# Pooled attention and two MLPs on one core: block 0's queries in 1 KB runs, five plain steps, and a plan with trace durations

## The chip, the cores and the metric

The kernel runs on 1 core of one Trainium2 chip. The metric is the device time of one execution in microseconds (us); three executions were timed, and the median counts. One further execution was profiled.

## The reference, cut to what matters

Attention over keys and values that are averaged in groups of 8, then two MLPs. Everything is float32.

```python
# q, k, v: 8 batches, 8 heads, 576 positions, 64 wide
k_p, v_p = mean of k and v over groups of 8 positions        # 72 pooled positions
attn = softmax(q @ k_p.T / 8);  x = attn @ v_p               # x: 4608 tokens x 512
h = x @ w_in                                                  # 512 -> 2048
g = where(h >= 1, h, where(h <= -1, 0, (h + 1) ** 2 / 4))
y = g @ w_out                                                 # 2048 -> 512
out = (sigmoid(y @ w_gate) * (y @ w_val)) @ w_out2            # 512 -> 1536 -> 512
```

## The kernel before, in words

The 4608 tokens are nine blocks of 512. Blocks 0 to 6 go through the first MLP one after the other, each in 16 steps (one step is 128 columns of `w_in` and the matching 128 rows of `w_out`). Blocks 7 and 8, and then the second MLP for all blocks but the first, are done in pairs with Strassen's seven products (lines 1000 to 1350). Attention for block j+1 and later is woven in between the steps of the blocks before.

**Precision.** Nearly every product is three matmuls (lines 607 to 611): each operand is split into a high part in fp32r and a low part (value minus high), and high times high, high times low and low times high are added in PSUM. The high part is a ScalarE copy, the low part a VectorE subtraction (lines 531 to 545, recorded at L534 and L543). The raw weights come from memory as 64-bit words whose two halves are put together by two ScalarE and four VectorE instructions per weight tile (lines 556 to 600).

**Plain steps.** In block 0, steps below `PLAIN = 12` (line 241) skip the split for the second product: `g` and the `w_out` rows stay float32 and one float32 matmul (line 772; the profile records it as two) takes the place of three. From step 12 on the step splits `w_out` into a `wj` buffer and `g` into two halves, so ScalarE makes two more copies and VectorE two more subtractions per step (lines 746 to 756).

**Block 0's attention** runs per pair of heads p = 0 to 3. `pooled` (line 319) loads keys and values, sums groups of 8 on VectorE or TensorE, turns the keys on TensorE (line 360) and scales them into `kt`. `unit` (line 385) loads the queries of the two heads with two DMAs (line 401) into a tile ordered (token, head, width), so each run that lands is 64 floats, 256 bytes; turns them with four TensorE transposes (line 407); makes scores (line 436), the maximum (line 445), exponentials with their sums (line 448), the division (line 455), turns the weights (line 470), multiplies with the values (line 508) and splits the result into x (lines 515 and 522). Block 0's q tiles of pairs 2 and 3 borrow the two `wj` buffers. All DMAs from SyncE go through one queue (SP), in the order of issue; GpSimd's own go through POOL's.

**Order of the work.** Nothing is written out by hand: every instruction is an `Op` with an engine, an estimated cost, a key (a due time) and its data dependencies, and `Plan.issue` (line 126) walks through a model of the engines, taking at each point the ready operation with the smallest key. An `Op` may have two ways, on ScalarE or VectorE, and the plan takes the one that ends first. The costs and the constants at the head of the file (lines 25 to 56) therefore change only the order of issue on each engine and that choice, not what one instruction does. A DMA ends in the model when its last byte lands (line 195).

**Rows out.** At the end of a first-MLP block the four accumulator banks are copied to two staging tiles (`out_rows`, line 621): the first is the single `st` tile, the second a tile of the `raw` pool (two buffers), which also takes the raw `w_out` rows, the second MLP's weights on their way to memory and the tiles of `prepare1`. From block 4 on, x is loaded from memory (line 706) into the `x` pool of eight tiles, which by then holds those of the two blocks before.

Of the kernel before, what the change touches and what calls it, by code (L numbers as in the profile page):

```python
# [27 lines left out]
RATE0, RAMP = 240e3, 30.0  # L28

START = 30.0  # L30
STEP1 = 6.35
# [16 lines left out]
PREP2 = 0.5  # L48
AHEAD_COPY = 8.0
UNIT0, UNIT_STEP = 14.0, 3.2  # L50
PREP0, PREP_STEP = (30.5, 68.5), 4.5
AHEAD_RELOAD = 30.0
BEHIND_V = 14.96
# [21 lines left out]
class Plan:  # L75
# [50 lines left out]
    def issue(self):  # L126
# [19 lines left out]
        while n:  # L146
# [42 lines left out]
            if o.bytes:  # L189
# [5 lines left out]
                free[eng], o.end = max(t, lanes[-8] + lat), lanes[-1]  # L195
# [12 lines left out]
def pooled_attention_two_mlps(  # L208
# [30 lines left out]
    PE_SUMS = 1  # L239
    DVE_VALUES = (2, 3)  # L240
    PLAIN = 12
# [37 lines left out]
    def fixed(t):  # L279
        return Buf(tile=t)  # L280
# [23 lines left out]

    T0, S1, S2 = START, STEP1, 7.8

    def due1(s):
        return T0 + S1 * s
# [10 lines left out]
    def pooled(b, p, T):  # L319
# [27 lines left out]
        load(k, ks, T - 20)  # L347
# [9 lines left out]
        else:  # L357
            kp = buf_a("kp", 2, [C, 2, D])
            pool_sum(T, ks, kp, b == 0)
            op(PE, 0.06 if b else 0.25, T + 1, lambda: nc.tensor.transpose(  # L360
                out=pt.t[:, 0:C], in_=kp.t.rearrange("c h d -> c (h d)"), identity=ident.t[:C, :C]),
                r=[kp, ident], w=[pt], share=C / P)


        op((ACT, DVE), (0.21, 0.22), T + 2, (
            lambda: nc.scalar.activation(out=kt.t[:, 0:C], in_=pt.t[:, 0:C], func=AF.Copy, scale=att_scale),
            lambda: nc.vector.tensor_scalar(
                out=kt.t[:, 0:C], in0=pt.t[:, 0:C], scalar1=att_scale, scalar2=None, op0=ALU.mult)), r=[pt], w=[kt])
        load(v, vs, T - (10 if b else AHEAD_V))
# [15 lines left out]
    def unit(j, p, T):  # L385
# [10 lines left out]
        if first:  # L396

            qb = buf_a("q", 2, [P, NT4, 2, D]) if p < 2 else Buf(wj_p, "wj", 2, [P, 2, TB])
            qs = Src(qb) if p < 2 else Src(qb, lambda t: t[:, 0].rearrange("p (t h d) -> p t h d", t=NT4, h=2))
            for h in range(2):  # L400
                op(SP, 0.475, T - 20, lambda h=h: nc.sync.dma_start(
                    out=qs()[:, :, h], in_=q[0, h0 + h, 0:TB].rearrange("(s t) d -> s t d", t=NT4)), w=[qb], nbytes=TB * D * 4)
            ptq = bank("acc")

            def transposes():
                for t in range(NT4):
                    nc.tensor.transpose(out=ptq.t[:, P * t:P * t + P],
                                        in_=qs()[:, t].rearrange("s h d -> s (h d)"), identity=ident.t)
            op(PE, 1.05, T, transposes, r=[qb, ident], w=[ptq])
# [3 lines left out]
        else:  # L413
# [8 lines left out]
            for f in range(4):  # L422
                op(SP, 0.475, T - 20, lambda f=f: load_q(f), w=[qs], nbytes=TB * 256, dmas=len(segs))
# [7 lines left out]

        def scores():
            for r0 in range(0, TB, D):
# [5 lines left out]
        op(PE, 1.15 if first else 0.6, T + 3, scores, r=[qT] + [kts[b % 2, p] for _, _, b, _ in segs], w=scs)  # L439
        for h in range(2):  # L440
# [6 lines left out]
            for t in range(NT4):  # L447
                op(ACT, 0.3 if first else 0.52, T + 5, lambda t=t, h=h, view=view, mx=mx: nc.scalar.activation(
                    out=e.t[:, t, h, 0:C], in_=view()[:, t], func=AF.Exp,
                    bias=mx.t[:, t:t + 1], scale=1.0,  # L450
                    accum_out=sums.t[:, t, h:h + 1]), r=[sc, mx], w=[e, sums], after=[zeros])
# [10 lines left out]
        if first:  # L462

            flat = Src(aT, lambda t: t.rearrange("c a h t j -> c (a h t j)"))
            for h in range(2):
# [5 lines left out]
                op(PE, 1.02, T + 9, transposes, r=[e, ident], w=[pt])  # L471
# [39 lines left out]
        op(PE, 1.05 if first else 0.86 + 0.25 * (len(segs) > 1 and j % 2), T + 18 - AHEAD_PX * first, values,  # L511
# [879 lines left out]
```

## Time and profile before

| | us |
|---|---|
| median of the three runs | 1690.37 |
| lowest and highest run | 1690.08, 1693.66 |
| the profiled execution's own time | 1693.15 |
| its span, first to last instruction | 1691.4 |
| TensorE busy in the span | 1667.2 (99%) |
| VectorE busy | 1168.6 (69%) |
| ScalarE busy | 967.8 (57%) |
| GpSimd busy | 238.3 (14%) |
| mean granted TensorE clock (1 is full) | 0.996 |

Busy time is the union of the instructions' recorded spans; instructions on one engine overlap a little, so the distance from start to start is what one costs in a dense stretch. The shares are means over stages with different limits, and the kernel has four: block 0's attention (until about 33 us), block 0's steps (until about 146 us), the other blocks of the first MLP, and the Strassen pairs.

### The profile page before, as it was taken

Reading aid. Unit: us, or ns where it says so; the run is one execution under the profiler, and the core shown is the slowest. Engines: PE = TensorE matmul, PEld = TensorE weight load, DVE = VectorE, ACT = ScalarE, POOL = GpSimd, SP = SyncE. Lnnn points to the kernel's source line nnn. Section 1 sums busy time; section 2 is a strip of 40 time slices with the busy share of each in tenths; the row PEclk is TensorE's granted clock in tenths of the full one; section 3 lists DMA queues with packets and bytes.
Section 4 is the critical chain, followed back from the end, with each engine's and each line's share of the span. In section 5 each row is a group of like instructions: output and inputs, shape, how many; then the busy total and the mean of one; then the engine's idle time right before and its main releaser. Section 6 shows DMA issues by size and latency. Waiting matters only on the chain.

```text
span 1691.4 us, 26119 instructions
## 1 busy us (share of the span) xinstructions
PE 1667.2 (99%) x8484; PEld 1323.8 (78%) x8484; DVE 1168.6 (69%) x2166; ACT 967.8 (57%) x2140; POOL 238.3 (14%) x338
## 2 busy tenths in 40 slices
PE   7999999999999999999999999999999999999998
PEld 5657777777777777788888888878888888888886
DVE  7988767878787878846778856574448445744476
ACT  6767556676676668643466735454435454544344
POOL 1224323333433222100000002100000000000000
PEclk8999999999999999999999999999999999999999
DMA  8889867777877656547887879997889788977774
GB/s 218 246 250 244 203 138 203 230 217 195 233 201 191 175 162 211 175 159 303 326 275 239 292 237 370 360 343 215 234 257 304 211 238 274 280 194 205 206 219 135
DMA packets 308647, 396.07 MB, mean 234 GB/s; under 512 B 133664, under 2 KB 173856, under 8 KB 306976
## 3 DMA queue, kind: packets, MB, share of 16 engines
q1 hardware_dynamic: 270848, 285.97, 57.1%
q0 software_dynamic: 37664, 108.44, 20.6%
q8 instruction: 68, 1.11, 0.3%
q14 instruction: 67, 0.55, 0.1%
HBM read 272.11 MB, written 112.72 MB: 228 GB/s over the span
## 4 chain that ended last, share of the span: by engine, by line
PE 89%; DMA 5%; DVE 3%; SPq 1%; ACT 1%; issue 1%; POOL 0%; DVEq 0%; POOLq 0%; ACTq 0%
PE acc L609 12%; PE h L609 12%; PE acc L611 12%; PE acc L610 12%; PE h L610 11%; PE h L611 11%; PE a L609 5%; PE a L611 5%; PE a L610 5%; PE a L508 2%; DMA kv<-in_k_dram 2%; PE a L436 1%; PE acc L772 1%; DMA raw<-in_moe_w_out_dram 1%; SPq L487 1%
## 5 line engine op out<-in xcount | busy, mean ns | idle before, releaser
L834 DVE TENSOR_TENSOR g<-win,g 128x512 fp32r<-128x512 f32 x168 | 114.8, 689 | 113.1 <-ACT g L833 111.7
L609 PE MATMUL h<-x,win 128*128 128x512 f32 x448 | 183.4, 409 | 2.1 <-DVE t L746 2.1
L611 PE MATMUL h<-x,win 128*128 128x512 f32 x448 | 175.1, 391 | 1.3 <-DVE win L543 1.3
L610 PE MATMUL h<-x,win 128*128 128x512 f32 x448 | 175.3, 391 | 0.4 <-DVE x L522 0.4
L833 ACT CAST g<-win 128x512 fp32r<-128x512 f32 x168 | 104.3, 624 | 111.8 <-PE acc L611 90.5
L609 PE MATMUL acc<-g,wj 128*128 128x512 f32 x400 | 161.3, 403 | 0.0
L610 PE MATMUL acc<-g,wj 128*128 128x512 f32 x400 | 156.5, 391 | 0.0
L611 PE MATMUL acc<-g,wj 128*128 128x512 f32 x400 | 156.2, 391 | 0.0
L609 PE MATMUL acc<-g,wo 128*128 128x512 f32 x360 | 140.1, 389 | 0.7 <-ACT g L833 0.7
L611 PE MATMUL acc<-g,wo 128*128 128x512 f32 x360 | 140.1, 389 | 0.0
L610 PE MATMUL acc<-g,wo 128*128 128x512 f32 x360 | 140.1, 389 | 0.0
L609 PE MATMUL h<-x,ws 128*128 128x512 f32 x336 | 131.3, 391 | 0.4 <-ACT h L1335 0.4
L610 PE MATMUL h<-x,ws 128*128 128x512 f32 x336 | 131.0, 390 | 0.2 <-DVE x L829 0.2
L611 PE MATMUL h<-x,ws 128*128 128x512 f32 x336 | 130.8, 389 | 0.0
L741 ACT ACTIVATE t<-h,half 128x512 f32<-128x512 f32 x112 | 77.2, 689 | 89.0 <-PE h L611 88.0
L609 PEld LDWEIGHTS h<-x,win 128*128 128x128 f32 x448 | 84.1, 188 | 28.4 <-issue 6.0
L611 PEld LDWEIGHTS h<-x,win 128*128 128x128 f32 x448 | 84.1, 188 | 20.7 <-DVE win L543 2.6
L610 PEld LDWEIGHTS h<-x,win 128*128 128x128 f32 x448 | 84.2, 188 | 19.2 <-issue 2.4
L609 PEld LDWEIGHTS acc<-g,wj 128*128 128x128 f32 x400 | 75.1, 188 | 24.3 <-issue 7.4
L611 PEld LDWEIGHTS acc<-g,wj 128*128 128x128 f32 x400 | 75.1, 188 | 16.8 <-DVE wj L543 0.3
L534 ACT CAST wj<-wout_f 128x512 fp32r<-128x512 f32 x100 | 61.8, 620 | 43.4 <-PE acc L611 37.1
L610 PEld LDWEIGHTS acc<-g,wj 128*128 128x128 f32 x400 | 75.1, 188 | 14.6 <-DVE f L590 0.2
(308 smaller groups left out, 4062.0 us busy)
## 6 DMA issues: line engine op xcount, KB each, us to landing
ws<-seven SPq DMA_DIRECT2D x412, 256.0 KB
wo<-seven_o SPq DMA_DIRECT2D x144, 256.0 KB
seven<-f POOLq DMA_DIRECT2D x64, 256.0 KB, 3.8
seven<-wa POOLq DMA_DIRECT2D x8, 1792.0 KB, 7.7
seven_o<-wo POOLq DMA_DIRECT2D x42, 256.0 KB, 5.8
w<-f POOLq DMA_DIRECT2D x36, 256.0 KB, 4.2
wo<-seven SPq DMA_DIRECT2D x36, 256.0 KB
win<-in_moe_w_in_dram SPq DMA_DIRECT2D x16, 512.0 KB
```

The source lines that it names most:

```text
L436: nc.tensor.matmul(out=scs[h].t[r0 % P:r0 % P + D, r0 // P * C:r0 // P * C + C], lhsT=qT.t[D * h:D * h + D, r0:r0 + D], rhs=kts[b % 2, p]. ...
L487: op(SP, 0.65, T + 10, lambda a=a, bl=bl, n=n: nc.sync.dma_start(out=aT.t[32 * bl:32 * bl + n, a].rearrange("c h t j -> c (h t j)"), in_=a ...
L508: nc.tensor.matmul(out=px.t[D * h:D * h + D, lo:hi], lhsT=vps[b % 2, p].t[:, h], rhs=rhs, start=True, stop=True)
L534: ACT: (0.52, lambda: nc.scalar.copy(out=dst.t[:, 0], in_=src())),
L609: nc.tensor.matmul(out=o, lhsT=wh, rhs=xh, start=start, stop=False, skip_group_check=more)
L610: nc.tensor.matmul(out=o, lhsT=wh, rhs=xl, start=False, stop=False, skip_group_check=more)
L611: nc.tensor.matmul(out=o, lhsT=wl, rhs=xh, start=False, stop=stop, skip_group_check=more)
L741: op(ACT, 0.69, Tg, lambda t=t, hps=hps: nc.scalar.activation(out=t.t, in_=hps.t, func=AF.Relu, bias=half.t, scale=0.5), r=[hps, half], w=[t])
L772: nc.tensor.matmul(out=accs[c].t, lhsT=wj.t[:, c * P:(c + 1) * P], rhs=g.t, start=m == 0, stop=m == M1 - 1)
L833: op2(ACT, cost, key, lambda: nc.scalar.copy(out=out_hi(), in_=val()), r=[src, b], w=[b])
L834: op2(DVE, cost, key + 0.5, lambda: nc.vector.tensor_tensor(out=out_lo(), in0=val(), in1=out_hi().bitcast(F32), op=ALU.subtract), r=[src, ...
```

## The change

- Block 0's queries are loaded with one DMA per pair of heads, into a tile ordered (head, token, width), in which the four tokens of a partition are one run of 1 KB. A transpose of 128 columns then holds two tokens of one head, not two heads of one token, so the keys are also put, by two matmuls, into a second set of 72 columns with the heads exchanged, and `first_scores` picks for each head and token parity the half that lies on the same rows. The number of score matmuls (16 per pair), of transposes and of exponentials stays.
- `PLAIN` goes from 12 to 5: steps 5 to 11 of block 0 get the split and three matmuls.
- The rows of blocks 0 to 4 are staged in two tiles of the `x` pool; those of block 5 both in `st`, one after the other. The reload of x for block j waits for the copies of block j-2's rows.
- The plan's costs are set to other values, a DMA ends 0.7 us later in the model, and the constants at the head get new values. Loops that add idle matmuls are there with a count of 0.

```diff
+LATE = 0.7
-RATE0, RAMP = 240e3, 30.0
+RATE0 = 240000.0
+RAMP = 23.86
-START = 30.0
-STEP1 = 6.35
+START = 30.317
+STEP1 = 6.332
...
-                free[eng], o.end = max(t, lanes[-8] + lat), lanes[-1]
+                free[eng], o.end = max(t, lanes[-8] + lat), lanes[-1] + LATE
...
-    PLAIN = 12
+    PLAIN = 5
...
-            kts[i, p] = fixed(ac.tile([P, P], F32, name=f"kt{i}{p}"))
+            kts[i, p] = fixed(ac.tile([P, C if i else 2 * C], F32, name=f"kt{i}{p}"))
...
+            def turn():
+                nc.tensor.transpose(out=pt.t[:, 0:C], in_=kp.t.rearrange("c h d -> c (h d)"), identity=ident.t[:C, :C])
+                if b == 0:
+                    for h in range(2):
+                        nc.tensor.matmul(out=pt.t[D - D * h:2 * D - D * h, C:2 * C], lhsT=kp.t[:, h], rhs=ident.t[:C, :C], start=True, stop=True)
...
-            qb = buf_a("q", 2, [P, NT4, 2, D]) if p < 2 else Buf(wj_p, "wj", 2, [P, 2, TB])
-            for h in range(2):
-                op(SP, 0.475, T - 20, lambda h=h: nc.sync.dma_start(
-                    out=qs()[:, :, h], in_=q[0, h0 + h, 0:TB].rearrange("(s t) d -> s t d", t=NT4)), w=[qb], nbytes=TB * D * 4)
+            qb = buf_a("q", 2, [P, 2, NT4 * D]) if p < 2 else Buf(wj_p, "wj", 2, [P, 2, TB])
+            op(SP, 0.475, T - 20, lambda: nc.sync.dma_start(
+                out=qs(), in_=q[0, h0:h0 + 2, 0:TB].rearrange("h (s t) d -> s h (t d)", t=NT4)), w=[qb], nbytes=TB * D * 8)
...
+        def first_scores():
+            kt = kts[0, p].t
+            for u in range(2):
+                for lo in (0, D):
+                    for h, odd in ((0, 0), (1, 1), (1, 0), (0, 1)):
+                        rows, i = slice(D * odd, D * odd + D), 2 * h + u
+                        nc.tensor.matmul(
+                            out=scs[odd].t[lo:lo + D, i * C:i * C + C], lhsT=qT.t[rows, i * P + lo:i * P + lo + D],
+                            rhs=kt[rows, (h ^ odd) * C:(h ^ odd) * C + C], start=True, stop=True)
...
-            st = buf_a("st", 1, [P, 2, TB]) if early and i == 0 else Buf(raw_p, "raw", 2, [P, 2, TB], fifo=None if early else True)
+            st = Buf(x_p, "x", 2 * KD, [P, 2, TB], fifo=None) if early > 0 else buf_a("st", 1, [P, 2, TB]) if early else Buf(raw_p, "raw", 2, [P, 2, TB])
...
-        out_rows(due1(s + 2) - 10, y_d[j].t, accs, [y_d[j]], j < NB1 - 1)
+        rows_of[j] = out_rows(due1(s + 2) - AHEAD_Y, y_d[j].t, accs, [y_d[j]], 1 if j + 2 < NB1 else -1 if j < NB1 - 1 else 0)
...
-            op(DVE, 0.69, Tg + 2, lambda t=t, hps=hps, o=o: nc.vector.scalar_tensor_tensor(
+            op(DVE, 0.61, Tg + 2, lambda t=t, hps=hps, o=o: nc.vector.scalar_tensor_tensor(
...
-                last_y[c] = [op(PE, 0.9 if plain else 0.65, due1(s + 2) + 2.6 + 0.1 * c, mm, r=[wj, g], w=[accs[c]], behind=last_y[c])]
+                last_y[c] = [op(PE, 1.03 if plain else 0.68, due1(s + 2) + 2.6 + 0.1 * c, mm, r=[wj, g], w=[accs[c]], behind=last_y[c])]
```

The other costs go the same way (VectorE's full-tile operations from 0.69 to 0.61, ScalarE's copies from 0.6 or 0.62 to 0.485 or 0.52, TensorE's products from 1.3 to 1.36), and so do the steps of the pairs (`PSTEP` from 27.3 to 28.262, `LEN2` from 114 to 115.884, `STEP2` from 7.8 to 7.682).

## Rows read from the trace of the kernel before

**Rows 1.** The page, busy time of each engine, and the granted clock in 40 slices.

```profile
PE 1667.2 (99%) x8484; PEld 1323.8 (78%) x8484; DVE 1168.6 (69%) x2166; ACT 967.8 (57%) x2140; POOL 238.3 (14%) x338
...
PEclk8999999999999999999999999999999999999999
```

**Rows 2.** Busy time by stretch of the span; the columns are in the first line.

```profile
core 0: us, PE busy (x) PEld busy (x) DVE busy (x) ACT busy (x) POOL busy (x), PEclk, DMA share, GB/s
0.00:14.00 14.00, 6.06 (x83) 4.65 (x83) 6.77 (x16) 3.56 (x10) 0.70 (x6) 1.00 0.83 216
14.00:33.36 19.36, 17.62 (x141) 13.18 (x142) 15.99 (x41) 17.13 (x77) 1.32 (x1) 0.65 0.85 205
33.36:145.93 112.57, 109.81 (x624) 68.09 (x622) 102.32 (x209) 81.17 (x204) 30.58 (x35) 1.00 0.89 248
145.93:700.00 554.07, 551.47 (x3324) 429.99 (x3323) 438.36 (x921) 371.41 (x992) 176.00 (x240) 1.00 0.72 197
700.00:1650.00 950.00, 946.51 (x4160) 779.20 (x4160) 580.60 (x946) 477.34 (x830) 29.67 (x56) 1.00 0.81 260
```

**Rows 3.** The same view, four shorter stretches.

```profile
15.74:28.70 12.96, 12.96 (x108) 10.05 (x109) 9.73 (x25) 11.27 (x57) 1.32 (x1) 0.50 0.75 165
...
33.36:70.19 36.83, 36.38 (x225) 21.61 (x223) 35.20 (x73) 28.10 (x76) 10.82 (x12) 1.00 0.90 255
70.19:145.93 75.74, 73.43 (x401) 46.48 (x400) 67.12 (x137) 53.07 (x129) 19.76 (x23) 1.00 0.88 245
124.16:146.47 22.31, 21.05 (x119) 14.29 (x118) 22.31 (x46) 16.96 (x42) 6.21 (x7) 1.00 0.98 253
```

**Rows 4.** Timeline of the first 18 us: start, us, engine, instruction, [idle before <-releaser].

```profile
1.24 1.32 SPq L401 DMA_DIRECT2D q<-in_q_dram  x2
...
6.36 1.01 SPq L330 DMA_DIRECT2D x<-in_k_dram  x1
...
12.17 0.69 DVE L339 TENSOR_TENSOR x<-x 72x512 f32<-72x512 f32 x1 [0.76 <-DMA x<-in_k_dram]
...
15.74 1.36 PE L436 MATMUL a<-kt,qT 64*64 64x72 f32 x32 [2.31 <-DVE kt L367]
```

**Rows 5.** DMA packets from 6 to 12 us, then from 12 to 14 us.

```profile
DMA packets 3330, 1.48 MB, mean 247 GB/s; under 512 B 2892, under 2 KB 3013, under 8 KB 3330
...
DMA packets 590, 0.69 MB, mean 347 GB/s; under 512 B 86, under 2 KB 477, under 8 KB 590
```

**Rows 6.** Timeline of TensorE: a plain step, then a step of three matmuls.

```profile
42.93 3.70 PE L772 MATMUL acc<-g,wout_f 128*128 128x512 f32 x8
46.06 0.79 PE L609 MATMUL h<-x,win 128*128 128x512 f32 x1
46.69 0.39 PE L610 MATMUL h<-x,win 128*128 128x512 f32 x1
46.92 0.40 PE L611 MATMUL h<-x,win 128*128 128x512 f32 x1
...
173.50 0.39 PE L609 MATMUL acc<-g,wj 128*128 128x512 f32 x1
...
176.22 0.39 PE L609 MATMUL h<-x,win 128*128 128x512 f32 x1
```

**Rows 7.** Timeline of VectorE: split subtractions, and block 2's first and last instruction before 145.93.

```profile
129.54 0.68 DVE L543 TENSOR_TENSOR g<-t,g 128x512 fp32r<-128x512 f32 x1
130.13 0.42 DVE L587 TENSOR_SCALAR f<-f 128x512 uint32<-128x512 uint32 x1
...
132.98 0.69 DVE L424 STREAM_TRANSPOSE qT<-q 128x512 f32<-128x512 f32 x1
...
145.80 0.18 DVE L454 RECIPROCAL sm<-sm 128x8 f32<-128x8 f32 x1
```

**Rows 8.** ScalarE's waits for weights, 33 to 135 us: total, times, longest.

```profile
ACT win L582 <- DMA win<-in_moe_w_in_dram: 4.9, 4, 2.8
ACT f L580 <- DMA raw<-in_moe_w_out_dram: 4.0, 4, 1.8
```

**Rows 9.** Timeline at the end of block 5: copies of the rows, and TensorE.

```profile
651.83 1.27 ACT L626 COPY st<-acc 128x512 f32<-128x512 f32 x2
...
666.75 0.68 DVE L627 COPY raw<-acc 128x512 f32<-128x512 f32 x1
```

More of the change, by code (lines that the diff above doesn't have):

```diff
@@ L47 @@
 MARK = 1, 7
-PREP2 = 0.5
+PREP2 = 0.732
 AHEAD_COPY = 8.0
[L50 to L53, printed above, removed]
+UNIT0 = 14.0
+UNIT_STEP = 3.2
+PREP0 = (30.5, 68.2)
+PREP_STEP = 4.5
+AHEAD_RELOAD = 32.76
+BEHIND_V = 17.175
+AHEAD_Q = 17.412
+AHEAD_K = 20.0
+AHEAD_V1 = 10.0
+AT_SC = 2.855
+AT_PX = 17.408
+AHEAD_Y = 9.383
+AHEAD_S = 6.0
+AHEAD_W2 = 3.667
+BEHIND_P = 20.0
 class Buf:
@@ L438, in scores @@
                         lhsT=qT.t[D * h:D * h + D, r0:r0 + D], rhs=kts[b % 2, p].t[D * h:D * h + D, 0:C], start=True, stop=True)
-        op(PE, 1.15 if first else 0.6, T + 3, scores, r=[qT] + [kts[b % 2, p] for _, _, b, _ in segs], w=scs)
+        op(PE, 0.75, T + AT_SC, scores, r=[qT] + [kts[b % 2, p] for _, _, b, _ in segs], w=scs)
         for h in range(2):
@@ L446, in unit @@
                 out=mx.t, in_=view(), op=ALU.max, axis=AX.X, negate=True), r=[sc], w=[mx])
[L447 to L451, printed above, removed]
+            for i in range(NT4):
+                t, hh = (2 * (i % 2) + h, i // 2) if first else (i, h)
+                op(ACT, 0.3, T + 5, lambda i=i, t=t, hh=hh, view=view, mx=mx: nc.scalar.activation(
+                    out=e.t[:, t, hh, 0:C], in_=view()[:, i], func=AF.Exp,
+                    bias=mx.t[:, i:i + 1], scale=1.0,
+                    accum_out=sums.t[:, t, hh:hh + 1]), r=[sc, mx], w=[e, sums], after=[zeros])
         op(DVE, 0.07, T + 8, lambda: nc.vector.tensor_scalar(
@@ L510, in values @@
                             start=True, stop=True)
-        op(PE, 1.05 if first else 0.86 + 0.25 * (len(segs) > 1 and j % 2), T + 18 - AHEAD_PX * first, values,
+        op(PE, 1.0 if first else 1.05 + 0.1 * (len(segs) > 1 and j % 2), T + AT_PX - AHEAD_PX * first, values,
            r=[aT] + [vps[b % 2, p] for _, _, b, _ in segs], w=[px], share=C / P)
@@ L630, in out_rows, with idle_columns @@
                 r=[st], w=d, nbytes=P * DM * 8)
+        return rows
     zeros = memsets()
-    xs_of = {}
+    def idle_columns(n, key):
+        b = bank("acc")
+        op(PE, n / 1200, key, lambda: nc.tensor.matmul(
+            out=b.t[:, 0:n], lhsT=ident.t, rhs=e_sb.t.rearrange("p t h c -> p (t h c)")[:, 0:n], start=True, stop=True),
+            r=[ident, e_sb], w=[b])
+    for _ in range(0):
+        idle_columns(TB, -5)
+    for _ in range(0):
+        idle_columns(256, 25)
+    xs_of, rows_of = {}, {}
     for p in range(NPAIR):
@@ L922, in mm @@
                       w.t[:, 0], w.t[:, 1], m == 0, m == M2 - 1)
-            last[c] = [op(PE, 0.65, key + 0.1 * c, mm, r=[w, g], w=[accs[c]], behind=last[c])]
+            last[c] = [op(PE, 0.68, key + 0.1 * c, mm, r=[w, g], w=[accs[c]], behind=last[c])]
     lasts = [[] for _ in range(4)]
@@ L1033, in mm @@
                               start and i == 0, i == MP - 1, not start)
-                chain[:] = [op2(PE, 1.3, key, mm, r=[w, g] + ([] if start or i else o), w=o, behind=chain)]
+                chain[:] = [op2(PE, 1.36, key, mm, r=[w, g] + ([] if start or i else o), w=o, behind=chain)]
                 if (n, i) == MARK:
@@ L1284, in mm @@
                                   start and k == 0, k == 1, not start)
-                    op(PE, 1.3, T + H * pos, mm, r=[w] + xx + ([] if start else [o]), w=[o])
+                    op(PE, 1.36, T + H * pos, mm, r=[w] + xx + ([] if start else [o]), w=[o])
                 def add(key, o, b, u):
-                    op2(DVE, 0.69, key, lambda: nc.vector.tensor_tensor(out=o.t, in0=b.t, in1=u.t, op=ALU.add),
+                    op2(DVE, 0.61, key, lambda: nc.vector.tensor_tensor(out=o.t, in0=b.t, in1=u.t, op=ALU.add),
                         r=[b, u], w=[o])
```

108 lines of the change are left out of this document (58 added, 50 removed).

## The prediction

> **What bounds the kernel now.** I read the page first, then the busy time by stretch, then the timelines and waits of the two stretches in which the change's own edits lie. The page shows TensorE busy for 1667.2 of 1691.4 us and its clock full everywhere but in the first slice [rows 1]. So time can come out in four ways only: TensorE work removed, TensorE's idle time, its half-speed time, or work moved off a path where another engine is the limit.
>
> By stretch [rows 2] TensorE is idle for 14.00 - 6.06 = 7.9 us up to 14 us, 1.7 us up to 33.36 us (the first matmul of the first MLP step), 2.8 us up to 145.93 us (block 0's steps), 2.6 us up to 700 us and 3.5 us up to 1650 us. Between 15.74 and 28.70 us it was busy without a gap, at a granted clock of 0.50, the 1.2 GHz level [rows 3]; it had sat idle 2.31 us just before [rows 4]. At the 2.4 GHz level the same work would fill half the stretch, so 6.5 us lie there in principle. The stretch from 145.93 us on is TensorE's to 99.6%, so little else can be won there.
>
> Block 0's steps are the stretch to look at with care. TensorE is busy 109.81 of 112.57 us, but VectorE has 102.32 us there too [rows 2], and from 124.16 to 146.47 us, where the last steps are no longer plain, VectorE is busy for 22.31 of 22.31 us and TensorE is not [rows 3].
>
> **The change, part by part.**
>
> *Queries in 1 KB runs.* From 6 to 12 us the DMA engines moved 1.48 MB in 3330 packets, 2892 of them under 512 B; from 12 to 14 us, with 86 such packets among 590, they moved 347 GB/s [rows 5]. The 2892 small packets are the queries (256 B each, 0.74 MB). At 347 GB/s the other 0.74 MB takes 2.1 us of the 6, so the small ones took 3.9 us, an estimate of 190 GB/s. All queries are 4 x 256 KB = 1.05 MB: 5.5 us at 190, 3.0 us at 347 GB/s. The keys of pair 3, which land last of what the first scores need (12.17 us [rows 4]), have three of the four pairs' queries ahead: 3/4 x 2.5 = 1.9 us. SP's own time points to the same size: two query DMAs take 1.32 us to issue, and the last key DMA is issued at 6.36 us behind six of them [rows 4]; with three fewer it goes about 3 x 0.6 = 1.8 us earlier. The two overlap; I take 2.0 us for the arrival.
>
> The Trainium skill, page "DMA: Bandwidth & Descriptors", section "Why small descriptors are slow (HBM only)", gives a fixed cost of about 3 cycles per packet, 11 cycles for 256 B. By that rule 1 KB goes from 44 to 35 cycles, a fifth less, and the arrival would come about 3/4 x 5.5 / 5 = 0.8 us earlier, not 1.9 (an estimate from that page). The row shows a far larger loss, and the sum goes by the row.
>
> How much of 2.0 us reaches the first step? What follows is a chain on ScalarE (17.13 of 19.36 us busy), VectorE (15.99) and TensorE at half clock (17.62) [rows 2], and each of these moves with its inputs. I take all of it, -2.0. Bounds: 0, if the plan's new order fills the gap with something else first; and -4.2, if the order also closes ScalarE's remaining 2.2 us.
>
> The new key halves add two 72-column matmuls per pair, eight in all, and the scaling copy grows from 72 to 144 columns. The nearest rows are the 32 records of one pair's scores, 1.36 us at half clock [rows 4]: 0.04 us each, 0.04 x 16 records = 0.7 us at the most, spread over four pairs and partly in the 2.3 us gap. Cost 0.2, bounds 0 and 0.7.
>
> *Seven steps out of plain.* A plain second product costs TensorE 46.69 - 0.23 - 42.93 = 3.53 us up to where the next matmuls run at their usual distance of 0.23; a split one 176.22 - 173.50 = 2.72 us [rows 6]. Seven steps save 7 x 0.81 = 5.7 us of TensorE. Each also gives VectorE two subtractions, 0.60 us from start to start [rows 7], so 7 x 1.2 = 8.4 us, and ScalarE two copies of about the same length, which its 31 free us [rows 2] hide; without that cover it would be as much again. VectorE is another matter: 102.32 + 8.4 = 110.7 us. Of this some belongs to block 2's attention and can wait: nine entries between the two shown, 3.9 us together [rows 7]. What must be done before step 16 is then 106.9 us, against 112.57 now. So VectorE, not TensorE (109.8 - 5.7 = 104.1), becomes the limit, and the gain is what VectorE's idle time leaves. It idled 4.4% from 33.36 to 70.19 us and not at all from 124.16 us on [rows 3]. At 4.4% the stretch takes 106.9 / 0.956 = 111.8 us (-0.8); at none, TensorE's own idle included, 106.9 (-5.7). Midway, 2.2%: 109.3 us, -3.3. What speaks for idle time staying is ScalarE's 4.9 + 4.0 us of waits for weights to land [rows 8]: a shorter stretch needs the same bytes sooner, with DMA at a share of 0.89 already [rows 2].
>
> *Rows in dead x tiles.* No instruction is added. It frees `raw` buffers of a row transfer at the ends of blocks 0 to 4. In block 5 both halves go through `st`, so the second copy waits for the first transfer. There the last copy runs today at 666.75 us, 14 us behind the first ones at 651.83 [rows 9], without an idle TensorE; a transfer in between is shorter than that, so it costs nothing. If that cover is gone, at most the 2.7 us of one second product [rows 6].
>
> *The new plan.* It changes the order from start to end. What it can win after 145.93 us is TensorE's 2.6 + 3.5 us of idle time [rows 2]. A plan that expects transfers later puts loads ahead; but the old order has left little. I take -1.0, with bounds -6.1 and +4.0 (as much again as two thirds of the idle time that this order left).
>
> The sum: -2.0 + 0.2 - 3.3 + 0 - 1.0 = -6.1 us. The profiled execution took 1693.15 us, 1.75 more than its span; less 6.1 it is 1687.05. It lies 2.8 us above the median of 1690.37, and from the median the forecast is **1684.3 us**. About 0.2% (3.4 us) is what a measurement here can tell from no change.
>
> **The rivals.**
>
> *VectorE takes over (slower).* Place: steps 5 to 15 of block 0. If VectorE keeps all of today's 10.25 us of idle time because it waits for weights, the stretch takes 106.9 + 10.25 = 117.2 us, +4.6, and TensorE idles for it. With the gain at the start lost in the same wait, 1690.4 + 4.6 = 1695.0. It decides above an idle time of 112.57 - 106.9 = 5.7 us. For it: VectorE's full stretch at the end, and the weight waits. Against: VectorE idled mostly where TensorE was the limit.
>
> *Hidden anyway.* Earlier keys and queries change only where TensorE waits: the half-clock stretch from 15.74 us takes them up, and the plain steps give the 0.8 us of the 4.4% case. 1690.4 - 0.8 = 1689.6. For it: between 15.74 and 28.70 us TensorE has no idle time left to lose. Against: all three engines of that stretch started from the late keys.
>
> *The full clock comes back early.* If denser arrivals spare TensorE the 2.31 us gap before 15.74 us, the clock need not fall, and the limit becomes ScalarE: 2.2 us more than the forecast. 1684.3 - 2.2 = 1682.1, and with the plain steps at VectorE's best another 2.4, 1679.7. The Trainium skill, page "TensorE: Matmul & The Clock Gate", section "What's actually happening", says that the throttled state is the default and that activity releases it. By that rule the stretch should have returned to the full clock soon; the trace shows 12.96 us of it, busy throughout, at 0.50, so here the rule does not carry, and I give this rival less than the others.
>
> *The change does not do what it says*: the plan could place the seven steps' splits so late that steps 5 to 11 run no sooner than plain ones. That is the hidden case and priced there.
>
> **How the numbers follow.** Forecast 0.45 (1680 to 1687, a tenth of it over 1687), full clock 0.15, hidden 0.20, VectorE 0.20. Faster by over 0.2% is below 1687.0: 0.40 + 0.15, and 0.03 for hidden cases in which the pairs give the idle time back: 0.58. Within: 0.05 + 0.17 = 0.22. Slower, above 1693.8: 0.20. The range runs from 1676, where the start's -4.2, the -5.7 and most of the late idle time come together, to 1696, VectorE's rival and 1 us of a worse plan. The faster cases' own range is 1678 to 1687.
>
> **What would show it.** Right: the last keys' first sum starts near 10.2 us, not 12.17; the first MLP matmul near 31.4; 40 records of L772 instead of 96; VectorE at 97 to 98% from there to step 16, which starts near 141; the distance from there to the end shorter by 1 us only. Wrong: VectorE idle over 5.7 us in block 0's steps with waits on weights, a first step still at 33 us, or new idle time of TensorE behind 145 us of more than 4 us.

## The result, and the profile after

The changed kernel takes **1703.43 us** (median of 7 runs, 1699.0 to 1707.55) against 1693.66 (7 runs, 1690.08 to 1698.16) in the same session: ratio 1.0063, 95% interval 1.0043 to 1.0083. It is slower, by about 10 us; forecast were 1684.3 and a range up to 1696. Its profiled span is 1701.3 us against 1691.4. First the page's busy line and clock line:

```profile
PE 1667.4 (98%) x8528; PEld 1333.7 (78%) x8528; DVE 1177.5 (69%) x2177; ACT 984.5 (58%) x2157; POOL 238.6 (14%) x338
...
PEclk9999999999999999999999999999999999999999
```

TensorE's busy time is that of [rows 1], 1667 us. So by this view the span's 9.9 us are idle time of TensorE. (Busy time is the union of records that overlap, 0.39 us long at a distance of 0.23 in [rows 6]; waits shorter than the overlap count as busy.) The busy time by stretch, cut as in [rows 2], says where:

```profile
0.00:14.00 14.00, 6.79 (x86) 5.32 (x86) 6.40 (x15) 5.26 (x20) 0.70 (x6) 1.00 0.84 222
14.00:33.52 19.52, 18.62 (x159) 14.04 (x155) 16.07 (x41) 16.17 (x66) 1.32 (x1) 1.00 0.76 164
33.52:147.76 114.24, 108.89 (x653) 75.31 (x650) 109.72 (x221) 87.71 (x215) 32.71 (x37) 0.97 0.87 251
147.76:700.00 552.24, 545.47 (x3296) 425.45 (x3295) 434.39 (x912) 374.78 (x991) 172.90 (x237) 1.00 0.72 196
700.00:1650.00 950.00, 942.32 (x4146) 776.90 (x4145) 578.03 (x940) 477.94 (x828) 30.94 (x58) 1.00 0.81 258
```

Idle is length minus TensorE's busy time: 5.4 us in block 0's steps (2.8 before), 6.8 up to 700 us (2.6), 7.7 up to 1650 us (3.5). At the start it is 8.1 against 9.7. Behind the first step, then, 11 us of new idle time. The waits behind block 0's steps, of the kernel before and of the changed one (us in total, times, longest):

```profile
PE h L609 <- DVE t L746: 2.1, 2, 1.8
PE a L609 <- ACT a L1335: 0.9, 2, 0.7
PE acc L609 <- ACT g L833: 0.7, 1, 0.7
```

```profile
PE h L643 <- DVE win L1370: 2.3, 2, 1.6
PE a L542 <- DMA aT<-aq: 2.1, 1, 2.1
PE a L645 <- DVE wa L875: 1.3, 1, 1.3
PE h L644 <- DVE x L875: 1.2, 1, 1.2
PE a L542 <- ACT e_sb L482: 1.1, 2, 0.8
PE a L542 <- DMA kv<-in_k_dram: 1.1, 1, 1.1
PE h L645 <- DVE wa L875: 1.1, 1, 1.1
```

No single wait is large. TensorE works its list in order, so each is a place where the plan put a matmul before its operand was there: in front of attention's small matmuls (L542 multiplies weights with values; `aT` are the attention weights turned by twelve DMAs) and of the Strassen pairs' first matmuls.

The start, in the timeline (compare [rows 4]), first the DMA issues and VectorE, then TensorE:

```profile
1.24 0.41 SPq L421 DMA_DIRECT2D q<-in_q_dram  x1
...
3.48 0.44 SPq L347 DMA_DIRECT2D x<-in_k_dram  x1
...
10.27 0.69 DVE L356 TENSOR_TENSOR x<-x 72x512 f32<-72x512 f32 x1 [1.57 <-DMA x<-in_k_dram]
...
13.62 0.28 DVE L356 TENSOR_TENSOR kp<-x 72x128 f32<-72x128 f32 x1
...
15.15 0.68 DVE L356 TENSOR_TENSOR x<-x 72x512 f32<-72x512 f32 x1
```

```profile
11.82 1.08 PE L427 MATMUL acc<-ident,wj 128*128 128x128 f32 x4 [1.18 <-DMA wj<-in_q_dram]
...
18.70 3.69 PE L396 MATMUL acc<-x,ident 72*72 72x128 f32 x16
...
26.94 1.08 PE L542 MATMUL acc<-aT,vp 72*64 72x512 f32 x4
...
28.85 1.91 PE L396 MATMUL acc<-x,ident 72*72 72x128 f32 x16
```

The last keys' DMA (pair 3's) is issued at 3.48 us (6.36 before). VectorE sums the keys of the pairs 0 to 3 in turn, three additions each, the last of them into `kp`. The sum that starts at 10.27 us is pair 2's, whose last addition runs at 13.62; in the kernel before pair 2's starts at 9.87. Pair 3's keys are first summed at 15.15 us, 3.0 us later than the 12.17 of [rows 4], and VectorE no longer waits for them there: the new plan puts other work first. Of the queries, the transposes of pair 2's now wait 1.18 us for theirs. Sixteen matmuls of one form take 3.69 us at 18.70 and 1.91 at 28.85, and the four at 26.94 already run at the pace of the later ones, so TensorE came back from its lower level only shortly before 26.94 us (the scores at 22.32 still took 1.29 us), although the clock column of that stretch says 1.00. The first MLP matmul starts at 33.52 us, no earlier than before.

### The profile page after: what moved, and what is told of

Read it like the earlier page. It is cut to its first block, busy times and chain, and to the rows that moved or that the text cites. A ratio compares the mean times of both kernels' runs of the same rounds, so it can differ in the third digit from the quotient of the medians.

```text
span 1701.3 us, 26196 instructions
## 1 busy us (share of the span) xinstructions
PE 1667.4 (98%) x8528; PEld 1333.7 (78%) x8528; DVE 1177.5 (69%) x2177; ACT 984.5 (58%) x2157; POOL 238.6 (14%) x338
## 4 chain that ended last, share of the span: by engine, by line
PE 80%; DMA 9%; DVE 4%; issue 3%; ACT 2%; SPq 1%; POOL 1%; POOLq 0%; DVEq 0%; ACTq 0%
PE acc L643 11%; PE acc L645 11%; PE acc L644 11%; PE h L643 11%; PE h L645 10%; PE h L644 10%; PE a L644 4%; PE a L645 4%; PE a L643 4%; DMA kv<-in_k_dram 2%; PE a L542 2%; DMA seven<-f 1%; DMA wa<-w 1%; PE a L469 1%; DMA raw<-w 1%
## 5 line engine op out<-in xcount | busy, mean ns | idle before, releaser
L643 PE MATMUL acc<-g,wj 128*128 128x512 f32 x428 | 171.7, 401 | 0.0
L645 PE MATMUL acc<-g,wj 128*128 128x512 f32 x428 | 167.1, 390 | 0.2 <-DVE wj L577 0.2
L644 PE MATMUL acc<-g,wj 128*128 128x512 f32 x428 | 167.2, 391 | 0.0
L645 PEld LDWEIGHTS h<-x,win 128*128 128x128 f32 x448 | 84.6, 189 | 21.5 <-DVE win L577 3.0
L792 DVE SCALAR_TENSOR_TENSOR t<-t,h 128x512 f32<-128x512 f32 x107 | 73.0, 682 | 38.7 <-ACT t L789 37.9
L643 PEld LDWEIGHTS acc<-g,wj 128*128 128x128 f32 x428 | 80.3, 188 | 24.5 <-issue 6.8
L645 PEld LDWEIGHTS acc<-g,wj 128*128 128x128 f32 x428 | 80.4, 188 | 18.2 <-DVE wj L577 0.8
L644 PEld LDWEIGHTS acc<-g,wj 128*128 128x128 f32 x428 | 80.4, 188 | 15.4
```

The lines of the kernel that those rows point to most:

```text
L643: nc.tensor.matmul(out=o, lhsT=wh, rhs=xh, start=start, stop=False, skip_group_check=more)
L644: nc.tensor.matmul(out=o, lhsT=wh, rhs=xl, start=False, stop=False, skip_group_check=more)
L645: nc.tensor.matmul(out=o, lhsT=wl, rhs=xh, start=False, stop=stop, skip_group_check=more)
L792: op(DVE, 0.61, Tg + 2, lambda t=t, hps=hps, o=o: nc.vector.scalar_tensor_tensor(out=o.t, in0=t.t, scalar=1.0, in1=hps.t, op0=ALU.min, op1 ...
```

## The experiments

Theories. *VectorE*: the steps out of plain make VectorE the limit of block 0. *Slack*, later called *margin*: the new costs are exact (an exponential at 0.3 us in place of 0.52) and so take away an unseen reserve, without which TensorE stands in front of attention. *Order*: any change of a number draws the instruction lists anew, and the list before is a lucky one. *Content* is its opposite: what the change says costs the time, whatever the order.

The summary stands first. "Idle" is TensorE's, by the view of busy time by stretch (length minus busy), from the first MLP matmul to step 16, on to 700 us, and on to 1680 us, in each run's profile.

| kernel | ratio to before (95%) | idle: block 0 | to 700 | to 1680 | sum |
|---|---|---|---|---|---|
| before | 1 | 2.8 | 2.6 | 4.2 | 9.6 |
| e18 before, new attention numbers | 1.0001 (0.9990 to 1.0011) | 2.1 | 1.2 | 3.2 | 6.5 |
| e8 before, new queries | 1.0016 (1.0006 to 1.0026) | 2.9 | 1.3 | 5.3 | 9.4 |
| e14 before, STEP1 6.40 | 1.0021 (1.0009 to 1.0034) | 3.3 | 2.1 | 3.2 | 8.7 |
| e13 before, START 29.5 | 1.0034 (1.0017 to 1.0050) | 2.5 | 3.3 | 4.2 | 10.1 |
| e5 before, STEP1 6.34 | 1.0034 (1.0019 to 1.0049) | 1.7 | 4.3 | 5.3 | 11.3 |
| e11 before, exp 0.3 | 1.0047 (1.0029 to 1.0064) | 0.5 | 3.5 | 11.6 | 15.6 |
| e12 before, 16 plain | 1.0049 (1.0030 to 1.0069) | 0.7 | 4.4 | 4.8 | 9.9 |
| e4 after, old plan | 1.0053 (1.0035 to 1.0072) | 7.9 | 4.3 | 3.0 | 15.2 |
| e1 before, 5 plain | 1.0082 (1.0062 to 1.0103) | 7.7 | 4.7 | 8.9 | 21.3 |
| e6 after, exp 0.52 | 1.0042 (1.0023 to 1.0061) | 9.0 | 0.6 | 7.3 | 17.0 |
| after | 1.0063 (1.0043 to 1.0083) | 5.3 | 6.8 | 8.4 | 20.5 |
| e17 after, aT cost 0.85 | 1.0067 (1.0051 to 1.0082) | 6.8 | 4.5 | 7.4 | 18.7 |
| e15 after, START 30.817 | 1.0073 (1.0058 to 1.0088) | 7.8 | 4.7 | 8.9 | 21.4 |
| e9 after, unchanged | 1.0079 (1.0051 to 1.0106) | 6.3 | 5.9 | 9.3 | 21.5 |
| e10 after, exp and pairs old | 1.0081 (1.0062 to 1.0100) | 10.3 | 1.2 | 9.9 | 21.4 |
| e3 before, new plan | 1.0087 (1.0066 to 1.0108) | 7.3 | 6.2 | 7.4 | 21.0 |
| e7 after, attention old | 1.0113 (1.0092 to 1.0133) | 9.9 | 2.9 | 11.8 | 24.5 |
| e2 after, 12 plain | 1.0114 (1.0094 to 1.0134) | 6.6 | 7.9 | 5.8 | 20.3 |
| e16 after, STEP1 6.382 | 1.0124 (1.0101 to 1.0146) | 6.3 | 12.0 | 8.2 | 26.5 |

The ratio follows the last column, roughly. From the least idle (e18, 6.5 us) to the most (e16, 26.5 us) there are 20 us, and between their ratios 1.23%, which is 20.8 us. Worked out against the kernel before (idle over 9.6 us, beside the ratio times 1691), the two agree within 4.5 us for all but e13 (5.3), e12 (7.9) and e2 (8.5). The profile is one execution and the ratio comes from several; against the span of the same profile (-4 to +21 us) the idle time agrees within 4.5 us in all of them.

In ten of the eighteen experiments below (e1, e2, e3, e4, e7, e10, e11, e12, e16, e18) the median lay outside every range that a theory had given for it. The theories sort the runs; they do not foretell a time.

### e1 to e4: one part alone, and all but one

e1 is the kernel before with `-PLAIN = 12` `+PLAIN = 5`.

> The kernel before with PLAIN = 5 and nothing else. VectorE theory (seven more steps with 1.2 us of subtractions each make VectorE the limit of block 0, and TensorE's gaps there cost more than the 5.7 us that it saves): not faster than before, 0 to +5 us, with the step-16 landmark at 146 to 149 us and VectorE at 95% or more between 33 and 146 us. Plan theory (only the new order costs): faster by 3 to 5 us.

1706.39 us. Its block 0 beside that of e12 below (same columns as above):

```profile
32.62:148.53 115.91, 108.21 (x653) 72.57 (x651) 108.50 (x221) 88.55 (x219) 33.08 (x39) 1.00 0.90 255
```

TensorE is busy 1.6 us less than in [rows 2], VectorE 6.2 us more, and the stretch is 3.3 us longer. VectorE released 6.4 of the 7.7 us for which TensorE idles there (1.7 of 2.8 before). The part from which I expected most costs time alone. But step 16 starts only 2.6 us later than before, and the profiled span is 14.2 us longer: most of the loss lies behind block 0, where this edit changes no work, only the order.

e2 is the changed kernel with `-PLAIN = 5` `+PLAIN = 12`.

> The changed kernel with PLAIN back at 12. VectorE theory: half or more of the loss comes back, 1694 to 1698 us, and no fall of the granted clock behind 33 us. Plan theory: still 1700 to 1704 us, since the waits behind step 16 stay.

1711.22 us, above both ranges. Going back to twelve plain steps does not bring the time back; with the new plan it costs time, and block 0 gets longer (118.56 us against 114.24, and 113.33 in e9).

e3 is the kernel before with the new costs, constants and `+LATE = 0.7` alone.

> The kernel before with the changed kernel's costs, constants and LATE, but its own query loads, PLAIN = 12 and rows. Plan theory: slower than before by 5 to 8 us, with the waits of the Strassen pairs (between 770 and 1130 us) as in the changed kernel. VectorE theory: within 3 us of before.

1707.13 us. The work is that of the kernel before (8484 records of TensorE in both); the order, and a few choices between ScalarE and VectorE, cost 15 us here. Block 0 of e3, then of e2:

```profile
30.18:151.01 120.83, 113.52 (x624) 69.73 (x622) 106.30 (x214) 82.90 (x207) 34.50 (x41) 0.97 0.91 254
```

```profile
29.44:148.00 118.56, 111.98 (x624) 69.50 (x622) 105.65 (x214) 82.87 (x206) 35.11 (x41) 0.99 0.90 254
```

The stretch is 8.3 us longer than before in e3, with VectorE idle for 14.5 us of it, not 10.25.

e4 is the changed kernel with `-LATE = 0.7`, the old costs and the old constants.

> The changed kernel's query loads, PLAIN = 5 and rows with the old costs and constants. Plan theory: within 3 us of before or faster. VectorE theory: slower than before by 3 to 6 us, most of it lost before step 24 (195 us in the kernel before).

1701.31 us, with only 3.0 us idle behind 700 us but 7.9 in block 0. The five plain steps alone (e1) cost 0.82%, the plan alone (e3) 0.87%, all of the change together 0.63%: the parts do not add. With the old plan, five plain steps lengthen block 0 (115.91 us in e1 and 117.57 in e4, against 112.57); with the new plan they shorten it (114.24, against 120.83 in e3 and 118.56 in e2). One list stands behind each of these numbers.

### e5 to e8: order, slack, and the queries

e5 is the kernel before with `-STEP1 = 6.35` `+STEP1 = 6.34`.

> The kernel before with STEP1 = 6.34 in place of 6.35: no edit to the work, only a new order (1117 of TensorE's 6893 listed lines move). Order theory (the order of before is an unusually good one, and any other costs some 10 us): slower by 5 to 15 us. Slack theory (the changed plan leaves attention too little time, so TensorE stands in front of its small matmuls): within 4 us of before, since the costs and due times are the old ones.

1698.58 us: a due time moved by 0.16%, with every instruction and cost as before, is worth 0.34%.

e6 is the changed kernel with the exponential's cost set back: `-op(ACT, 0.3, T + 5` `+op(ACT, 0.3 if first else 0.52, T + 5`.

> The changed kernel with one cost put back: an exponential of blocks 1 and later counts 0.52 us in the plan, not 0.3. Slack theory: 3 to 6 us faster than the changed kernel (1697 to 1700 us), with TensorE's waits in front of attention matmuls (9.6 us in the changed kernel's trace, 1.6 before) under 6 us. Order theory: 1700 to 1708 us, with waits elsewhere.

1697.71 us. Idle between block 0 and 700 us falls from 6.8 to 0.6, as slack would have it; in block 0 it rises to 9.0. The ratio, 1.0042, is below the changed kernel's 1.0063, but their intervals overlap.

e7 goes on from e6: `-AHEAD_Q = 17.412` `-BEHIND_V = 17.175` `-AT_PX = 17.408` `+AHEAD_Q = 20.0` `+BEHIND_V = 14.96` `+AT_PX = 18.0`, and the old costs of scores and values.

> The changed kernel with attention's old due times and costs as well (queries 20 us ahead in place of 17.4, values 18 us behind in place of 17.4, exponentials 0.52). Slack theory: 1692 to 1698 us, and the waits in front of attention matmuls under 4 us. Order theory: 1700 to 1708 us.

1710.37 us. More reserve for attention should have gained more; the idle stays high in block 0 (9.9) and rises in the pairs (11.8, from 7.3 in e6). This is a miss for slack.

e8 is the kernel before with the new loads of the queries and the new score matmuls alone.

> The kernel before with block 0's queries in 1 KB runs and the keys in both orders, and nothing else. Start theory of the forecast: 1 to 2 us faster than before, first MLP matmul at 31.4 us. Hidden: first MLP matmul at 33 us or later, time within 3 us of before. Order theory: slower by 5 us or more, lost behind 33 us.

1693.48 us, 0.16% over its own before: the hidden case by its time, and neither a gain nor order's loss of 5 us. This run keeps the old plan, so it shows the new loads by themselves. VectorE still waits for pair 3's keys:

```profile
11.28 0.69 DVE L340 TENSOR_TENSOR x<-x 72x512 f32<-72x512 f32 x1 [0.69 <-DMA x<-in_k_dram]
```

They are summed 0.9 us earlier than before, not 2.0; the first MLP matmul starts at 32.34 us, 1.0 us earlier; and step 16 at 145.63, 0.3 us earlier.

### e9 to e12: the change again, the pairs, the exponential, the other way

e9 is the changed kernel, not a line different.

> The changed kernel once more, not a line different, for what differs between two executions of one program. Its first profile had TensorE at the lower level up to some 30 us and its first MLP matmul at 33.5 us; two kernels with the same start (e2, e6) had it at 29.4 and 29.8. If the order of the instructions settles where TensorE stands, the idle in front of the attention matmuls is again near 9.9 us and that behind 700 us near 8.9, with the same waits at the same instructions, and the median lies within 0.2% of 1703. If the early clock is what the time hangs on, an execution with the first step near 29.5 us ends some 4 us earlier than one with it at 33.5.

1705.57 us. Three waits of TensorE in the timeline of the first profile, and the same three in this one:

```profile
170.37 1.08 PE L542 MATMUL a<-aT,vp 72*64 72x128 f32 x8 [2.05 <-DMA aT<-aq]
...
770.94 0.50 PE L645 MATMUL a<-x,wa 128*128 128x512 f32 x1 [1.25 <-DVE wa L875]
...
1098.76 0.50 PE L643 MATMUL h<-win,ws 128*128 128x512 f32 x1 [1.57 <-DVE win L1370]
```

```profile
167.11 1.98 PE L542 MATMUL a<-aT,vp 72*64 72x128 f32 x8 [2.06 <-DMA aT<-aq]
...
769.64 0.50 PE L645 MATMUL a<-x,wa 128*128 128x512 f32 x1 [1.18 <-DVE wa L875]
...
1098.15 0.50 PE L643 MATMUL h<-win,ws 128*128 128x512 f32 x1 [2.09 <-DVE win L1370]
```

The waits belong to the list of instructions, not to the execution. This one had its first MLP matmul at 31.12 us, 2.4 us earlier, and its span ended 1.5 us later (1702.8): the time does not hang on the start alone.

e10 goes on from e6 with the old numbers of the pairs: `-STEP2 = 7.682` `-PSTEP = 28.262` `+STEP2 = 7.8` `+PSTEP = 10.5 * 2.6`, and the old costs there.

> The changed kernel with the old exp cost (as e6) and, beside it, the old costs and steps for the second part, the pairs of MLP rows. Slack theory: the old, larger costs keep the pairs' TensorE work away from its copies, the idle behind 700 us falls from 7.8 us (e6) to 4 to 6, and the median to 1694 to 1697. Order theory (each list of instructions has its own idle, no single cost carries it): anything from 3 to 11 us of idle there, and a median of 1693 to 1703 with no relation to the cost.

1705.55 us, 9.9 us idle behind 700 us. A miss for slack, and the time is above order's range too: the pairs' own old numbers do not take away the pairs' waits.

e11 is the kernel before with `-op(ACT, 0.3 if first else 0.52, T + 5` `+op(ACT, 0.3, T + 5`.

> The kernel before with one number changed, the exp's cost in the later blocks from 0.52 to 0.3, which is what the instruction takes. Slack theory: the idle in front of the attention matmuls rises from 1.6 us to 6 or more and the time by 4 to 8 us (1695 to 1699). Order theory: a rise of 0 to 8 us like that of e5 (1698.6), but the added idle may lie anywhere, with the attention's share at 1 to 4 us. If exact costs help, it is 2 us or more below the kernel before.

1700.53 us, but the idle up to 700 us is 3.5 and that of the pairs 11.6 (4.2 before): most of the added time is not in front of attention. More for order than for slack.

e12 is the kernel before with `-PLAIN = 12` `+PLAIN = 16`.

> The kernel before with 16 plain steps instead of 12: four more steps at some 3.8 us of TensorE in place of 3.0, and less on VectorE by four times the split step's share. TensorE theory (my prediction's 0.47 us a step for the change from plain to split, run the other way): step 16 comes 1.9 us later and the time is up by 1.9 to 3.2 us. VectorE theory: step 16 is bound by VectorE's stream, so it comes at 145.9 us or up to 2 us earlier, and the time is at most 1 us from the kernel before.

1697.4 us. Its block 0:

```profile
32.91:144.30 111.39, 110.66 (x617) 66.45 (x614) 102.80 (x208) 78.23 (x198) 33.17 (x39) 1.00 0.90 256
```

With more plain steps (the second products of two of the four fall before step 16) TensorE is busy 0.85 us longer and the stretch is 1.2 us shorter than before. The landmark is where VectorE's theory put it, but TensorE idles 0.7 us here and VectorE 8.6, so this run does not show VectorE as the limit. The total is up by 0.49%, from behind step 16, where neither theory expected it.

### e13 to e16: the order redrawn in both kernels

e13 and e14 are the kernel before with `+START = 29.5` and with `+STEP1 = 6.40`; e15 and e16 the changed one with `+START = 30.817` and with `+STEP1 = 6.382`.

> The kernel before with START at 29.5 in place of 30.0: the same instructions and costs, another order (2513 lines of TensorE's list differ). Order theory: a draw like e5, 1693 to 1706 us, with idle time of TensorE at places where the kernel before has none. Content theory: within 0.3% of the kernel before, 1686 to 1696 us.

> The kernel before with STEP1 at 6.40 in place of 6.35 (1001 lines of TensorE's list differ). Order theory: 1693 to 1706 us. Content theory: 1686 to 1696 us.

> The changed kernel with START at 30.817 in place of 30.317 (1174 lines of TensorE's list differ). Order theory: a draw from the same range as that of before's family, 1693 to 1706 us, and not the idle times of the changed kernel at the same instructions. Content theory: 1700 to 1707 us, as the changed kernel in both of its runs.

> The changed kernel with STEP1 at 6.382 in place of 6.332 (623 lines of TensorE's list differ). Order theory: 1693 to 1706 us. Content theory: 1700 to 1707 us.

1696.81, 1694.22, 1703.82 and 1711.8 us. The three redrawn lists of before (with e5) lie 0.21 to 0.34% above it: its own list is a good one, worth about 0.3%. Their idle sums (8.7 to 11.3 us) hardly differ from its 9.6, so where it gains is not shown. The changed kernel and its two lists lie at 0.63 to 1.24%; the ratios of the families do not overlap, though the interval of e13 (up to 1.0050) reaches that of the changed kernel (from 1.0043). So both theories may hold a share, as far as three lists each can tell: some 5 us of the loss (0.3%) would be the lucky list of before, the rest content. In the slowest list (e16) the waits in front of the values matmul are longer yet:

```profile
PE a L542 <- DMA aT<-aq: 6.1, 2, 3.9
PE a L542 <- ACT e_sb L482: 5.1, 3, 2.6
```

That this path waits here, and not in the redrawn kernels of before, led to the last two runs.

### e17 and e18: is the attention path the cause?

e17 is the changed kernel with a true cost of the twelve DMAs: `-op(SP, 0.65, T + 10` `+op(SP, 0.85, T + 10`.

> The changed kernel with one cost raised, that of each of the twelve DMAs which turn a pair's attention weights, from 0.65 to 0.85 (a group of twelve took 7.6 to 10.9 us in its trace, 0.63 to 0.91 each), so that the plan puts the values matmul some 2.4 us later behind them. Margin theory: the waits of the values matmul for aT and the exponentials (4.6 us of the 9.9 in front of attention) fall to 1 us or less, and the time by 3 to 6 us, to 1697 to 1701. Rival (the waits only mark a plan that is too tight in general): those waits go, as many come elsewhere, and the time stays at 1701 to 1706.

1700.24 us, ratio 1.0067. By the ratio nothing changed (1.0063 and 1.0079 without the edit); the median falls in margin's range, since four of the six executions took 1699.5 to 1700.5 us and two 1705.7 and 1706.0, so the time does not decide. The profile is of one of the two slower ones. Its waits behind block 0's steps:

```profile
PE h L643 <- DVE win L1370: 2.2, 1, 2.2
PE a L379 <- DVE kp L356: 1.8, 1, 1.8
PE a L542 <- ACT e_sb L482: 1.6, 2, 1.3
PE h L643 <- DVE gs L1358: 1.4, 1, 1.4
```

The wait for `aT` is gone, that for the exponentials is not, and others stand in place of the first; the idle sum is 18.7 us against 20.5. That is nearer to the rival.

e18 is the kernel before with `+AHEAD_V = -9.162`, `+BEHIND_V = 17.175`, exp 0.3, and loads, scores and values at the new costs and due times.

> The kernel before with the new plan's attention numbers alone: exp 0.3, the queries' loads 2.6 us later, scores and values a little earlier and at their new costs, the values' sums 2.2 us later. Margin theory: the waits of the values matmul for aT and the exponentials, nowhere over 0.5 us in the kernel before and its three redrawn orders, appear here with 2 us or more, TensorE's idle time in front of attention rises from 1.6 us to 6 to 14, and the time to 1697 to 1704. Rival: idle in front of attention stays at 1.5 to 4 us, and the time within the redrawn orders of before, 1693 to 1699.

1691.02 us against 1690.55, ratio 1.0001; its stretch up to 700 us:

```profile
145.05:700.00 554.95, 553.73 (x3336) 432.78 (x3335) 443.48 (x930) 376.85 (x994) 172.33 (x237) 1.00 0.72 198
```

With the new attention numbers TensorE idles 1.2 us there, less than before. In this list, with the rest of the old plan, the tight attention path costs nothing: by itself it is not the cause.

**What is shown, and what stays open.** Shown: the loss stands, by the view of busy time, in TensorE's idle time behind the first step; the waits come back at the same instructions when the same list runs again (e9); the new plan's numbers alone cost 0.87% (e3), with the work of the kernel before; and whether five plain steps help block 0 depends on the plan. No repair of one wait (e6, e7, e10, e17) made the kernel faster clear of the noise. Argued only: that VectorE is the limit of block 0 with five plain steps (most of TensorE's waits there are for it in e1, but both engines idle over 7 us), and how much of the loss is the good list of before. Open: which of the plan's remaining numbers (the transfers' 0.7 us, the costs of the MLP's own operations) carries its share, and whether e1 to e4, one list each, are typical; their orders were not redrawn. No version here beats the kernel before; e18 equals it.

## Why the prediction was wrong, point by point

*Arrival of the keys: mis-sized, and the hit is luck.* Predicted was 10.2 us, and a sum of keys does start at 10.27. But that is pair 2's (9.87 before), and with the new plan and the old loads it starts at 10.45 us (e3). Pair 3's keys are summed at 15.15 us. Where the old plan still waits for them, they come at 11.28 (e8) and 12.48 (e4), against 11.83 to 13.53 in the eight kernels with the old loads and an old plan. The size of 2.0 us came from the small packets' rate in [rows 5]; by the rule of the Trainium skill, page "DMA: Bandwidth & Descriptors", section "Why small descriptors are slow (HBM only)", the gain was 0.8 us and the sum would have run at 11.4 (an estimate from that page). The 0.9 us of e8 lies nearer to that than to the row; one profile each does not settle the size.

*First MLP matmul: wrong in the first profile.* Predicted 31.4; measured 33.52, with 33.36 before. The step that failed is "I take all of it": its own bound of 0, the plan filling the gap with something else first, is what the sum at 15.15 us shows. The nine profiles with the changed kernel's start, e2, e6, e7 and e10 among them, lie from 28.95 (e16) to 34.0 us (e17); e3, with the old loads, had 30.18. So the plan and the clock move the start more than the loads do. In e16 the 32 score matmuls at 11.37 us took 0.78 us, in the first profile those at 12.83 took 1.29. That is the rival of the full clock, come true in e16 and in e6 (0.78 us at 12.11). It does not decide the time: e16 is the slowest kernel of all, e6 the fastest of the changed ones.

*Passing the start's gain on, -2.0: wrong.* In the first profile, e9, e15, e16 and e17 step 16 starts at 147.76, 144.45, 148.29, 144.23 and 149.99 us (145.93 before), behind first steps at 33.52, 31.12, 31.26, 28.95 and 34.0: an early start reaches it in e9 and e16, not in e15. And e9, 1.5 us ahead of the kernel before at that point, ends 11.4 us behind it (1702.8 against 1691.4).

*Seven steps out of plain, -3.3: wrong against the kernel before.* Measured 114.24 - 112.57 = +1.7, in e9 +0.8. Two terms failed. One is the credit of 3.9 us for block 2's attention "that can wait". Groups of VectorE in block 0's steps, before and after:

```profile
L481 DVE STREAM_TRANSPOSE aq<-e_sb 128x384 f32<-128x384 f32 x8 | 4.2, 557 | 0.0
L424 DVE STREAM_TRANSPOSE qT<-q 128x512 f32<-128x512 f32 x6 | 4.2, 700 | 0.0
L445 DVE TENSOR_REDUCE mx<-a 128x4 f32<-128x288 f32 x10 | 4.1, 447 | 0.5 <-PE a L436 0.5
```

```profile
L577 DVE TENSOR_TENSOR g<-t,g 128x512 fp32r<-128x512 f32 x10 | 6.8, 684 | 0.2 <-ACT g L568 0.2
L577 DVE TENSOR_TENSOR wj<-wout_f,wj 128x512 fp32r<-128x512 f32 x10 | 6.8, 681 | 0.8 <-ACT wj L568 0.8
L478 DVE TENSOR_REDUCE mx<-a 128x4 f32<-128x288 f32 x10 | 4.3, 451 | 0.6 <-PE a L469 0.5
L515 DVE STREAM_TRANSPOSE aq<-e_sb 128x384 f32<-128x384 f32 x8 | 4.2, 559 | 0.0
L444 DVE STREAM_TRANSPOSE qT<-q 128x512 f32<-128x512 f32 x5 | 3.5, 706 | 0.1
```

Of these groups the plan moved one query transpose; ten reductions and eight turns stayed. Without the credit my own step gives 102.32 + 8.4 = 110.7 us of VectorE; measured are 109.72, 2.8 more than the 106.9 of the prediction. The other is the idle time: 4.5 us (4%), not 2.2%. I took the middle between 4.4% and none and passed over the stretch between, from 70.19 us on, where [rows 3] has 8.6 of VectorE's 10.25 us of idle time. TensorE's own saving, 5.7 us in the prediction, shows as 0.9 us of busy time (2.8 in e9, 1.6 in e1); why is open. The rival "VectorE takes over" had this place, but its price of +4.6 us and its idle time over 5.7 did not come in the first profile; in e15 the stretch is 4.5 us longer, with 4.9 us idle. And the comparison with the kernel before mixes in the plan: under the new plan the seven steps gain some 4 us in block 0 (114.24 against 118.56 in e2).

*Rows in dead x tiles, 0: right.* TensorE has no wait over 0.3 us between 585 and 770 us, a stretch in which block 5 ends.

*The new plan, -1.0 with bounds -6.1 and +4.0: wrong, and the largest error.* Behind step 16 the idle went up by 8.4 us (from 2.6 + 4.2 to 6.8 + 8.4, up to 1680 us), and e3 shows the plan's numbers alone at +0.87% (15 us), with block 0 8.3 us longer behind a first step 3.2 us earlier, a stretch that the term did not look at. I bounded its harm by "as much again as two thirds of the idle time that this order left", which no row supports: an upper bound had to come from how much TensorE can idle in another order, not from how little it did in this one.

*Sign and chance.* I gave slower 0.20, all of it to VectorE. The new order, which touched all 1690 us, deserved a rival of its own.

## What to carry to other kernels

When one engine is busy for 98.6% of the span and its list comes from a planner, the present list is partly luck: move one due time by a per cent, measure a few lists, and judge a change against that spread (here 0.2 to 0.34% up from the list before), not against the one list. A repaired wait proves little by its own disappearance; look at the sum of the engine's idle time, which followed the span of its own profile here to within 4.5 us over changes of -4 to +21 us. Test a part under the plan it was made for: five plain steps lost time in block 0 with one plan and won it with the other. Credit deferrable work only where something in the plan makes it defer. And before a landmark in the trace counts as a hit, check that it is the same work: here pair 2's sum stood where pair 3's was expected.

## What the hardware showed that was not expected

The same idle time does not always cost the clock. In both profiles of the changed kernel TensorE waits for block 1's first queries, 1.67 and 1.69 us. The timeline of the first profile, then that of e9:

```profile
40.62 1.24 PE L469 MATMUL a<-kt,qT 64*64 64x72 f32 x32 [1.67 <-DVE qT L444]
```

```profile
38.20 0.73 PE L469 MATMUL a<-kt,qT 64*64 64x72 f32 x32 [1.69 <-DVE qT L444]
```

And the busy time of the 6 us around, in the same order (the granted clock is the third column from the end):

```profile
38.00:44.00 6.00, 4.33 (x43) 3.27 (x42) 5.31 (x12) 3.91 (x12) 1.96 (x2) 0.72 0.72 188
```

```profile
36.00:42.00 6.00, 4.31 (x48) 3.21 (x47) 5.97 (x12) 4.14 (x15) 1.93 (x2) 1.00 0.97 277
```

In the first the clock was at the 1.2 GHz level for part of the 6 us (0.72 over them) and the 32 matmuls took 1.24 us; in the second it stayed at 2.4 GHz and they took 0.73. Later it is the other way round: behind 2.05 us of idle time the eight matmuls at 170.37 us of the first profile took 1.08 us, behind 2.06 those at 167.11 of e9 took 1.98. The clock's return at the start differs in the same way. Two lines of e9, then one of e16:

```profile
10.96 1.29 PE L459 MATMUL h<-kt,qT 64*64 64x72 f32 x32
...
24.52 1.08 PE L542 MATMUL acc<-aT,vp 72*64 72x512 f32 x4
```

```profile
11.37 0.78 PE L459 MATMUL h<-kt,qT 64*64 64x72 f32 x32
```

The scores still take 1.29 us at 20.44 in e9, so its full level comes between there and 24.52 us; e16 has it at 11.37 (and is at the lower one again by 18.21, where scores take 1.29 us, behind a wait of 1.37 us in front of 15.70). The Trainium skill, page "TensorE: Matmul & The Clock Gate", section "What's actually happening", says that activity releases the throttle; both profiles agree that it is released, but with TensorE as busy in the one as in the other up to there (4.91 of the 5.30 us from 6 to 11.3 us), the moments lie some 10 us apart or more.

The clock column can be wrong for a stretch: from 14 to 33.52 us of the first profile it says 1.00, while sixteen matmuls of one form took 3.69 us at 18.70 and 1.91 at 28.85. There the durations tell the level.
